# Grouped-query attention on one core: TensorE's whole program put into one loop, with a first turn in which every operation is jumped over

## The chip, the cores and the metric

One core of a Trainium2 chip runs the kernel. The metric is the device time of one execution in microseconds (us); smaller is better. Five engines work side by side, each through its own instruction stream, and wait for each other by semaphores: TensorE (PE; its weight loads are PEld), VectorE (DVE), ScalarE (ACT), GpSimd (POOL) and SyncE (SP), which here only issues transfers. Sixteen DMA engines move data between the device's memory and the on-chip buffers, and also bring the engines' instructions.

## What is computed

```python
B, Hq, Hkv, Sq, Sk, D = 16, 32, 8, 16, 2048, 128        # q, k, v in bfloat16
k = jnp.repeat(k, rep, axis=1)                          # rep = 4
v = jnp.repeat(v, rep, axis=1)
scores = jnp.einsum("bhqd,bhkd->bhqk", q, k) * D ** -0.5
p = softmax(scores, axis=-1)
return jnp.einsum("bhqk,bhkd->bhqd", p, v)
```

K and V are 67 MB each; every one of the 128 pairs of batch and KV head has 64 query rows (4 heads of 16).

## The kernel before

**Tiling.** Four (batch, KV head) pairs are a quad; there are `NQD` = 32 quads. A quad is worked in two steps of two pairs each, so there are `NT` = 64 steps. Four quads share one load of Q (`NQC` = 8). Per quad one K load of 2048 KB and two V loads of 1024 KB are made. K has 3 buffers (`NK`), V has 4 (`NV`), the probabilities transposed (`PT`) have 4, the output 8.

**A step on the engines.** VectorE transposes K blocks on the fly (`kt`, L450: two instructions of 1.2 us a step) into `KT`. TensorE's operation S (L362 to L375) multiplies them with the transposed Q into `S_ps`: 32 matmuls, 16 with a weight load of their own (L372) and 16 on weights already loaded (L317). VectorE negates, scales and takes the maximum (`negated`, L463), and makes the bias (L472). ScalarE takes exp into `P` (L579). TensorE's PT (L392) transposes `P` into `ST_ps` in 8 instructions, and ScalarE evicts them (L591). TensorE's PV (L421) multiplies with V into `O_ps`: 64 matmuls, each with a weight load. ScalarE scales the finished quad by the reciprocal sum ("norm", L602), POOL packs it (L198), and SP stores it. Q (L350) is TensorE's transposition of a new Q group, after VectorE or POOL has laid it out (L178), once in eight steps.

**TensorE's order.** `pe_step(p)` gives S of step p+2, a Q in one step out of eight, PV of step p-5 and PT of step p-1. The program has three parts: `head` (warm-up matmuls W of no use to the result, Q of group 0, and the steps that have no PV yet) as straight code; a loop of `TURNS` = 8 turns with eight steps each; and the PV of the last quad as straight code. The loop's first instruction is put on slot `HEAD` = 82 of a 256-instruction block of the code. Within the loop the semaphores' values come from registers set at the start of each turn (L434 to L436). `in_last` names the operations that the last turn has too; the others lie within `pe.If_lt(...)` and are jumped over then (L438). VectorE has a loop of its own for nine turns (L505).

**What orders the transfers.** SP works through a fixed list: for each t it issues a Q load, a K load (even t), V loads, and later stores. A wait at one of them holds back all that stand behind it. A K load of quad n waits until VectorE has transposed quad n-3 (L248). A V load of quad n waits until TensorE has done PV of quad n-4 (L255). The K loads of quads 0 to 2 wait for nothing; that of quad 3 (t = 6) waits for VectorE's first two `kt` pairs, which need no TensorE work; that of quad 4 (t = 8) waits for the transposes in VectorE's steps 0 and 1, each of which stands behind an S.

**The end.** The last quad's V comes in three transfers over the keys 0 to 15, 16 to 27 and 28 to 31 (`LASTV`, `sem_vl`), its PV goes to `S_ps` in place of `O_ps` (`o_ap`, L165 to L168), and the last norms are shared between VectorE and ScalarE.

Of the kernel before, what the change touches and what calls it, by code (L numbers as in the profile page):

```python
# [7 lines left out]
ALU = mybir.AluOpType  # L8
# [5 lines left out]
NV = 4  # L14
# [7 lines left out]
PVLAG = 5  # L22
# [4 lines left out]
TURNS = 8  # L27
HEAD = 82
WARM = (7, 22, 6, 6, 6)
RING = 6  # L30
NMBASE = 8
EXPBASE = 3
VLOOP = (3, 30)
VHEAD = 140
LASTV = ((0, 16), (16, 28), (28, 32))


def bass_standalone__gqa_softmax__sampling_kernel(
# [13 lines left out]
    assert NQD % 4 == 0 and PVLAG == 5 and 8 * TURNS == NT and NQC == TURNS  # L52
# [71 lines left out]
    def pe_step(p):  # L124
        ops = [("S", p + 2)]
        if p >= PVLAG and (p + 3) % 8 == 0:
            ops += [("Q", (p + 3) // 8, b) for b in range(2)]
        if p >= PVLAG:
            ops.append(("PV", p - PVLAG))
        if p >= 1:  # L130
            ops.append(("PT", p - 1))
        return ops

    head = [("W", 0), ("Q", 0, 0), ("Q", 0, 1), ("W", 1), ("S", 0), ("W", 2), ("S", 1), ("W", 3), ("S", 2), ("W", 4)]
    head += pe_step(0)[1:]
    for p in range(1, PVLAG):
        head += pe_step(p)
    L = NT - 4
    turn_ops = [op for p in range(PVLAG, PVLAG + 8) for op in pe_step(p)]

    def in_last(op):
        e = 8 * (TURNS - 1)
        if op[0] == "Q":
            return op[1] + TURNS - 1 < NQC
        return op[1] + e < (NT - 2 if op[0] == "PV" else NT)

    tail = [("PV", NT - 2), ("PV", NT - 1)]

    act_prog = [("qe", 0, 0), ("qe", 0, 1)]
    for p in range(NT - 3):  # L150
# [5 lines left out]
        if p >= 1:  # L156
# [3 lines left out]
                 ("pe", L + 3, 0), ("norm", NQD - 1, 0)]  # L160
# [4 lines left out]
    def o_ap(n, x):  # L165
        if n != NQD - 1:
            return O_ps[:, 512 * x:512 * x + 128]
        return S_ps[:, 512 * x:512 * x + 128]  # L168
# [33 lines left out]
    with nc.Block() as block:  # L202

        @block.gpsimd
        def _(gp):
# [18 lines left out]
            gp.tensor_tensor(fold[:, :, :], half_m[:, :, 0, :], half_m[:, :, 1, :], op=ALU.add).then_inc(sem_id, 1)  # L224
            gp.sem_inc(sem_nm, NMBASE)
# [18 lines left out]
        def _(sp):  # L244
# [6 lines left out]
            def load_v(p):  # L251
                n, c = divmod(p, 2)
                s = n % NV
                if n >= NV and c == 0:
                    sp.wait_ge(sem_pv, 2 * (n - NV) + 2)  # L255
                if n < NQD - 1:
                    dst = Vb[s][:, c, :, :].rearrange("a j d -> a (j d)")
                    sp.dma_start(dst, vf[p]).then_inc(sem_v[s][c], 16)
                    return
                if c == 0:  # L260
                    return
                for x, (lo, hi) in enumerate(LASTV):
                    dst = Vb[s][:, :, lo:hi, :].rearrange("a c j d -> a c (j d)")
                    src = vf[p - 1:p + 1, :, 128 * lo:128 * hi].rearrange("c a x -> a c x")
                    sp.dma_start(dst, src).then_inc(sem_vl[x], 16)
# [8 lines left out]
            def store(n):  # L274
                s = n % NO
                if n < PAIRED:
                    sp.wait_ge(sem_pc, 2 * n + 2)
                elif n < NQD - 2:
                    sp.wait_ge(sem_nm, NMBASE + 2 * n + 2)
                elif n == NQD - 2:  # L280
                    sp.wait_ge(sem_nl, 3)
                else:
                    sp.wait_ge(sem_nm, NMBASE + 2 * (NQD - 2) + 1)
                    sp.wait_ge(sem_nl, 4)
                for c in range(2 if n < NQD - 1 else 1):
                    store_part(sp, n, c)

            for t in range(NT + SLAG):
                if t == 4:
                    sp.sem_inc(sem_exp, EXPBASE)  # L290
                    sp.sem_inc(sem_e2, TURNS - 1)
                for c in range(NQC):
                    if t == (QLOAD[c] if c < len(QLOAD) else 8 * c - QLEAD):
                        load_q(c)
                if t < NT and t % 2 == 0:
                    load_k(t // 2)
                for p in range(NT):
                    if t == p + VLAG[p >= VFAR]:
                        load_v(p)
                if t >= SLAG and t % 2 == 0:  # L300
                    store((t - SLAG) // 2)
# [4 lines left out]
        def _(pe):  # L306
            regs = {}

            def wait(s, value, slope, turn):
                pe.wait_ge(s, regs[slope, value] if turn else value)  # L310

            def held(turn):
                if turn:
                    pe.wait_ge(sem_id, 10)
# [10 lines left out]
            def emit(op, turn=False):  # L325
                if op[0] not in ("PT", "W"):
                    held(turn)
                if op[0] == "W":
                    if op[1] == 0:
                        pe.wait_ge(sem_id, 3)  # L330
                    w = ident4[:, :].bitcast(BF16)
                    x = w.unsqueeze(1).to_broadcast([128, 2, 256])
                    dst = O_ps[:, 0:512].rearrange("p (t q) -> p t q", t=2)
                    pe.matmul(dst, w[:, 0:128], x, start=True, stop=True)
                    for _ in range(WARM[op[1]] - 1):
                        matmul_on_loaded(dst, w[:, 0:128], x, (0, 0), True, True, (128, 128))
                elif op[0] == "Q":
                    _, c, b = op
                    if b == 0:
                        if c == 0:  # L340
                            pe.wait_ge(sem_id, 10)
                        wait(sem_q4, 4 * c + 4, 4, turn)
                    if c >= 1:
                        wait(sem_ev[b], 8 * c - 4, 8, turn)
# [8 lines left out]
                elif op[0] == "S":  # L353
                    _, n = op
                    wait(sem_kt, n + 1, 8, turn)
                    if n >= 1:
                        wait(sem_max, n, 8, turn)
                    c, i = divmod(n // 2, 4)
                    if n % 8 == 0:
                        wait(sem_qe, 2 * c + 2, 2, turn)  # L360
# [15 lines left out]
                elif op[0] == "PT":  # L376
                    _, h = op
                    if h % 2 == 0:
                        wait(sem_exp, EXPBASE + h + 2, 8, turn)
                    if h % 8 == 7:  # L380
                        wait(sem_e2, h // 8 + 1, 1, turn)
                    for i in range(2):
                        if h >= 4 and h % 8 == 4:
                            if i == 0:
                                wait(sem_qe, 2 * (h // 8) + 4, 2, turn)
                        elif h >= 1:
                            wait(sem_ev[i], h, 8, turn)
# [6 lines left out]
                elif op[0] == "PV":  # L394
                    _, h = op
                    n, half = divmod(h, 2)
                    if h < NT - 2:
                        wait(sem_ev[1], h + 1, 8, turn)
                    else:
                        for i in range(2):  # L400
                            wait(sem_ev[i], h + 1, 8, turn)
                    if n < NQD - 1 and half == 0:
                        for c in range(2):
                            wait(sem_v[n % NV][c], 16 * (n // NV + 1), 16, turn)
                    if half == 0:
                        if n == NQD - 1:
                            wait(sem_max, NT, 8, turn)
                        else:
                            wait(sem_nm, NMBASE + 2 * n, 8, turn)
                    pt = PT[h % NPT][:, :, :].bitcast(BF16).rearrange("p t (c q e) -> p t e c q", c=2, e=2)  # L410
                    for j in range(16):
                        key = 16 * half + j
                        if n == NQD - 1:
                            for x, (lo, _) in enumerate(LASTV):
                                if key == lo:
                                    pe.wait_ge(sem_vl[x], 16)
# [10 lines left out]
            for op in head:  # L427
                emit(op)
            PE = mybir.EngineType.PE
            for slope, values in ((8, range(1, 21)), (16, (16,)), (4, (8,)), (2, (4,)), (1, (1,))):  # L430
                for value in values:
                    regs[slope, value] = pe.alloc_register(f"r_{slope}_{value}")
            with nc.Fori(0, TURNS, 1, engines=[PE], head_slot={PE: HEAD}) as m:
                for (slope, value), r in regs.items():  # L434
                    pe.reg_alu(r, m, slope, ALU.mult)
                    pe.reg_alu(r, r, value, ALU.add)  # L436
                for kept, ops in groupby(turn_ops, in_last):
                    with nullcontext() if kept else pe.If_lt(regs[8, 1], 8 * (TURNS - 1) + 1):  # L438
                        for op in ops:
                            emit(op, True)  # L440
            for op in tail:
                emit(op)

        @block.vector
        def _(dve):
# [29 lines left out]
            def step(n):  # L475
# [7 lines left out]
                if x == 1:  # L483
                    dve.wait_ge(sem_max, n + 1)
# [18 lines left out]
            r_n = [dve.alloc_register(f"r_n{x}") for x in range(6)]  # L503
            r_k = [dve.alloc_register(f"r_k{x}") for x in range(2)]
            with nc.Fori(V0 // 3, V1 // 3, 1, engines=[VE], head_slot={VE: VHEAD}) as i:  # L505
                dve.reg_alu(r_n[0], i, 6, ALU.mult)
                dve.reg_alu(r_n[0], r_n[0], 1, ALU.add)
                for x in range(1, 6):
# [4 lines left out]
                for n in range(6):  # L513
# [6 lines left out]
                    if x == 1:  # L520
                        dve.wait_ge(sem_max, r_n[n])
# [28 lines left out]
            dve.wait_ge(sem_e2, TURNS)  # L550
# [4 lines left out]
            norm(NQD - 2, (0, 1), sem_nl)  # L555
# [3 lines left out]
        def _(act):  # L559
            for op in act_prog:  # L560
# [31 lines left out]
                elif op[0] == "free":  # L592
                    act.wait_ge(sem_ev[1], op[1] + 1)
# [10 lines left out]
            act.wait_ge(sem_nm, NMBASE + 2 * (NQD - 2) + 1)  # L604
            act.wait_ge(sem_nl, 4)
# [29 lines left out]
```

## Time and profile before

| | |
|---|---|
| three runs | 337.61, 337.77, 337.82 us; median 337.77 |
| the profiled execution | 337.53 us; span of the trace 335.7 us |
| busy share of the span | DVE 92%, PE 83%, ACT 66%, PEld 47%, POOL 31% |
| `KT` on DVE (L450) | 128 instructions, mean 1218 ns |
| `Sneg` on DVE (L463) | 128 instructions, mean 1205 ns |
| TensorE's first matmul, first Q, first S | 1.86, 5.30, 11.64 us |
| Q, K and V loads, median from issue to landing | 16.1, 18.2, 21.4 us |
| last V loads issued | 315.96 to 317.9 us |

The profiled execution is one execution; its span runs from the first to the last record. A timeline row has the start, the time over all its instructions, engine and line, the operation with out<-in, the count (x), and in brackets the idle time before it and what ended it; "issue" means that the engine waited for nothing that the profile shows. A row of the issue list (SPq) is the time at which SP issues a transfer, not when it lands. A wait row has the time in total, the number of times and the longest. A queue row has packets, MB, and the time that its packets took as a share of sixteen DMA engines over the stretch asked for. Register, branch and semaphore instructions have no rows among the engines' work.

### The profile page before, as it was taken

The numbers are of one execution on the slowest core, as the hardware profiler recorded it, in microseconds if no ns is written. First come the engines' busy times: TensorE is split into PE (matmuls) and PEld (weight loads), VectorE is DVE, ScalarE is ACT, GpSimd is POOL, SyncE is SP. The second block draws the span as 40 slices with busy tenths as digits, with TensorE's granted clock in tenths as the row PEclk, the third lists the DMA queues.
The fourth block names the chain that finished last, engine by engine and source line by source line (L and its number), as shares of the span: only waits on it lengthen the run. The fifth ranks groups of instructions, "written<-read, shape, count | busy, mean of one in ns | idle before, by whom it ended". The sixth has DMA issues, their size and how long they took to land.

```text
span 335.7 us, 14448 instructions
## 1 busy us (share of the span) xinstructions
PE 280.0 (83%) x6959; PEld 158.3 (47%) x5893; DVE 308.0 (92%) x465; ACT 220.6 (66%) x331; POOL 104.1 (31%) x98
## 2 busy tenths in 40 slices
PE   7877678888988899888988898878877979777895
PEld 2013344445545555455644554444543545444575
DVE  1999998998999999999999999899999999999872
ACT  2044666766787677766777677756767757567671
POOL 3840037300680029400680029400592000000000
PEclk9999999999999999999999999999999999999999
DMA  7999999999999999999999999999999999999995
GB/s 293 443 418 428 424 416 412 423 424 426 415 420 418 424 431 422 423 428 417 414 428 427 424 424 414 422 427 429 422 419 420 423 427 428 420 427 412 422 411 177
DMA packets 21151, 138.62 MB, mean 413 GB/s; under 512 B 3728, under 2 KB 7568, under 8 KB 9104
## 3 DMA queue, kind: packets, MB, share of 16 engines
q1 hardware_dynamic: 20992, 138.39, 99.3%
q8 instruction: 9, 0.15, 0.2%
q10 hardware_dynamic: 144, 0.03, 0.1%
q14 instruction: 6, 0.05, 0.0%
HBM read 136.31 MB, written 2.10 MB: 412 GB/s over the span
## 4 chain that ended last, share of the span: by engine, by line
DVE 49%; DMA 28%; PE 17%; issue 3%; ACT 2%; DVEq 0%
DMA Kn<-in_k_dram 27%; DVE Sneg L463 25%; DVE KT L450 22%; PE S_ps L372 5%; PE S_ps L317 4%; PE O_ps L421 3%; PE ST_ps L392 2%; PE ST_ps L350 2%; ACT P L579 1%; PE O_ps L317 1%; DMA Qn<-in_q_dram 1%; PE S_ps L421 1%; DVE Q L178 1%; ACT PT L591 0%; DVE nbias L472 0%
## 5 line engine op out<-in xcount | busy, mean ns | idle before, releaser
L450 DVE STREAM_TRANSPOSE KT<-Kn 128x1024 f32<-128x1024 f32 x128 | 151.0, 1218 | 10.3 <-DMA Kn<-in_k_dram 10.3
L463 DVE TENSOR_SCALAR_CACHE_REDUCE Sneg<-S_ps 128x1024 f32<-128x1024 f32 x128 | 149.9, 1205 | 4.9 <-PE S_ps L317 4.4
L579 ACT ACTIVATE P<-Sneg,nbias 128x2048 bf16<-128x2048 f32 (+1 forms) x66 | 129.0, 1955 | 15.4 <-DVE nbias L472 15.2
L372 PE MATMUL S_ps<-KT,QT 32*64 32x512 bf16 x1024 | 106.5, 387 | 35.4 <-DVE Sneg L463 34.4
L591 ACT ACTIVATE PT<-ST_ps 128x512 f32<-128x512 f32 x123 | 66.7, 597 | 60.2 <-PE ST_ps L392 60.2
L317 PE MATMUL S_ps<-KT,QT 32*64 32x512 bf16 x1024 | 106.0, 381 | 0.0
L178 POOL TENSOR_SCALAR Q<-Qn,mask 128x1024 bf16<-128x1024 bf16 x28 | 79.2, 2842 | 48.3 <-PE ST_ps L350 42.2
L372 PEld LDWEIGHTS S_ps<-KT,QT 32*64 32x64 bf16 x1024 | 34.8, 103 | 104.3 <-issue 91.3
L421 PEld LDWEIGHTS O_ps<-Vb,PT 64*64 64x64 bf16 x3968 | 58.0, 107 | 49.1 <-issue 48.7
L421 PE MATMUL O_ps<-Vb,PT 64*64 64x128 bf16 x3968 | 67.9, 218 | 14.4 <-DMA Vb<-in_v_dram 12.4
L198 POOL COPY O<-O 32x256 bf16<-32x256 bf16 x56 | 22.0, 393 | 163.9 <-ACT O L602 145.7
L392 PE MATMUL ST_ps<-ident,P 128*128 128x128 f32 x512 | 69.9, 280 | 0.2 <-ACT P L579 0.2
L392 PEld LDWEIGHTS ST_ps<-ident,P 128*128 128x128 f32 x512 | 54.8, 141 | 8.4 <-issue 2.6
L602 ACT ACTIVATE O<-O_ps,rrec 128x128 bf16<-128x128 f32 x56 | 17.5, 363 | 22.1 <-PE O_ps L421 22.1
L567 ACT ACTIVATE QT<-ST_ps 128x512 bf16<-128x512 f32 x14 | 7.7, 595 | 9.1 <-PE ST_ps L350 9.0
L579 ACT ACTIVATION_READ_ACCUMULATOR P<-Sneg,nbias 128x1 f32 x66 | 13.3, 201 | 0.0
L350 PEld LDWEIGHTS ST_ps<-fold,Q 128*128 128x128 bf16 x256 | 8.5, 101 | 7.9 <-issue 7.9
L317 PE MATMUL O_ps<-ident 128*128 128x512 bf16 x42 | 11.2, 415 | 0.0
L463 DVE DVE_READ_ACCUMULATOR Sneg<-S_ps 128x1 f32 x128 | 10.5, 82 | 0.0
L350 PE MATMUL ST_ps<-fold,Q 128*128 128x32 bf16 x256 | 9.4, 198 | 0.3 <-DVE Q L178 0.3
L472 DVE TENSOR_TENSOR nbias<-nhalf 128x2 f32<-128x2 f32 x32 | 5.3, 167 | 1.1
L459 DVE RECIPROCAL rrec<-rowsum 128x2 f32<-128x2 f32 x31 | 4.9, 159 | 0.0
(27 smaller groups left out, 19.9 us busy)
## 6 DMA issues: line engine op xcount, KB each, us to landing
Kn<-in_k_dram SPq DMA_DIRECT2D x32, 2048.0 KB, 18.2
Vb<-in_v_dram SPq DMA_DIRECT2D x63, 1024.0 KB, 21.4
Qn<-in_q_dram SPq DMA_DIRECT2D x8, 256.0 KB, 16.1
out_dram<-O SPq DMA_DIRECT2D x63, 32.0 KB, 19.8
Vb<-in_v_dram SPq DMA_DIRECT2D x1, 768.0 KB, 14.4
Vb<-in_v_dram SPq DMA_DIRECT2D x1, 256.0 KB, 14.6
out_dram<-O ACTq DMA_DIRECT2D x1, 32.0 KB, 2.0
```

The source lines that it names most:

```text
L178: eng.tensor_scalar(Q4[:, :, :, r, :].rearrange("p j b x -> p (j b) x"), src, mask[:, r:r + 1], None, op0=ALU.mult,).then_inc(sem_q4, 1)
L198: eng.tensor_copy(Osb[n % NO][64 * c:64 * c + 32, :, 1, :], Osb[n % NO][64 * c + 32:64 * (c + 1), :, 0, :],).then_inc(sem_pc, 1)
L317: return pe.add_instruction(mybir.InstMatmult(name=nc.get_next_instruction_name(), engine=mybir.EngineType.PE, ins=[pe.lower_ap(rhs), pe.l ...
L350: ins = pe.matmul(dst[:, j // 2, j % 2, e], src[:, j, b, e, :], fold[:, :, :], start=True, stop=True)
L372: ins = pe.matmul(s_ap, w, x, start=(acc == 0), stop=(acc == 3))
L392: ins = pe.transpose(dst[:, 128 * z:128 * (z + 1)], src[:, t, :], ident4[:, :])
L421: ins = pe.matmul(o_ap(n, x)[64 * c:64 * (c + 1), :], w[rows, c], Vb[n % NV][rows, c, key, :], start=(key == 0), stop=(key == 31),)
L450: ins = dve.transpose(KT[n % NKT][:, :].rearrange("p (t b g e a) -> p e g t b a", t=8, b=2, g=2, e=2)[:, e], Kn[Q % NK][:, :].bitcast(F32) ...
L463: ins = dve.tensor_scalar(Sneg[p % NS][:, 1024 * x:1024 * (x + 1)].rearrange("p (t a m) -> p t a m", t=8, m=4), S_ps[:, 1024 * y:1024 * (y ...
L579: ins = act.activation(P[n % 2][:, lo:hi, x, :].bitcast(BF16), Sneg[p % NS][:, 128 * lo:128 * hi].rearrange("p (t k) -> p t k", k=128), AC ...
L591: act.activation(pt_ap(h, i), stage_ap(h, i), ACT.Copy).then_inc(sem_ev[i], 1)
L602: act.activation(Osb[n % NO][:, x, 0, :], o_ap(n, x), ACT.Copy, scale=col(rrec, 2 * n + x)).then_inc(sem_nm, 1)
```

## The change

1. `head` and the tail go into the loop. The loop now begins three steps earlier in each turn's order (S of step 8t-1, Q of group t, PV of step 8t-8, and so on), and the order of the operations that are carried out stays the same. Turn 0 carries out what was `head`, turn 8 what was the end. Operations that belong to the turn's own group of steps are jumped over when `ended` is set, those of the group before when `started` is not. The warm-ups stand within the loop and are carried out in turn 0 alone. The loop starts on slot 0 of a block of code.
2. The loop runs ten times. In the first time the turn number is 15 (m + 15, cut to four bits), which sets `ended` and clears `started`: every operation is jumped over. Then turns 0 to 8 follow.
3. Since every wait takes its value from a register now, semaphores are given a base: `sem_max` 1, `sem_ev` 8, `sem_vl` 112, `sem_e2` 7, added by POOL and SP at their start. Seven of eight S drop their wait on the transposed K (`sem_kt`), which the wait on `sem_max` implies.
4. The last quad's V comes in four transfers: keys 0 to 15 as two (one for each half of the quad, on `sem_v`), then 16 to 27 and 28 to 31 as before. Its PV goes to `O_ps` like all others, and so waits for both norms of quad 30; of these ScalarE now does one and VectorE one, where VectorE did both.

```diff
-TURNS = 8
-HEAD = 82
+TURNS = 9
+HEAD = 0
...
     def pe_step(p):
         ops = [("S", p + 2)]
-        if p >= PVLAG and (p + 3) % 8 == 0:
-            ops += [("Q", (p + 3) // 8, b) for b in range(2)]
...
+        if p == 2 - PVLAG:
+            ops += [("Q", 0, b) for b in range(2)]
+        return ops + [("PV", p - PVLAG), ("PT", p - 1)]
...
-    turn_ops = [op for p in range(PVLAG, PVLAG + 8) for op in pe_step(p)]
+    turn_ops = [op for p in range(2 - PVLAG, 10 - PVLAG) for op in pe_step(p)]
...
     def o_ap(n, x):
-        if n != NQD - 1:
-            return O_ps[:, 512 * x:512 * x + 128]
-        return S_ps[:, 512 * x:512 * x + 128]
+        return O_ps[:, 512 * x:512 * x + 128]
...
-                for x, (lo, hi) in enumerate(LASTV):
+                for y in range(2):
+                    sp.dma_start(Vb[s][:, y, 0:16, :].rearrange("a j d -> a (j d)"),
+                                 vf[p - 1 + y, :, 0:2048]).then_inc(sem_v[s][y], 16)
+                for lo, hi, done in ((16, 28, sem_vl[0]), (28, 32, sem_vl[1])):
...
-                    wait(sem_kt, n + 1, 8, turn)
-                    if n >= 1:
-                        wait(sem_max, n, 8, turn)
+                    wait(sem_max, MAXBASE + n, 8)
...
                     if n % 8 == 0:
-                        wait(sem_qe, 2 * c + 2, 2, turn)
+                        wait(sem_kt, n + 1, 8)
+                        wait(sem_qe, 2, 2)
...
-            for op in head:
-                emit(op)
...
-            with nc.Fori(0, TURNS, 1, engines=[PE], head_slot={PE: HEAD}) as m:
+            with nc.Fori(0, TURNS + 1, 1, engines=[PE], head_slot={PE: HEAD}) as m:
+                pe.reg_alu(turn, m, 15, ALU.add)
+                pe.reg_alu(turn, turn, 15, ALU.bitwise_and)
+                pe.reg_alu(ended, turn, 8, ALU.bitwise_and)
+                pe.reg_alu(started, turn, 7, ALU.add)
+                pe.reg_alu(started, started, 8, ALU.bitwise_and)
                 for (slope, value), r in regs.items():
-                    pe.reg_alu(r, m, slope, ALU.mult)
+                    pe.reg_alu(r, turn, slope, ALU.mult)
                     pe.reg_alu(r, r, value, ALU.add)
-                for kept, ops in groupby(turn_ops, in_last):
-                    with nullcontext() if kept else pe.If_lt(regs[8, 1], 8 * (TURNS - 1) + 1):
+                with pe.If_eq(regs[8, 1], 1):
+                    pe.wait_ge(sem_id, 3)
+                    warm_up(WARM[0])
+                for first, ops in groupby(turn_ops, lambda op: op[1] >= 0):
+                    with pe.If_eq(ended, 0) if first else pe.If_ne(started, 0):
                         for op in ops:
-                            emit(op, True)
-            for op in tail:
-                emit(op)
+                            emit(op)
+                            if op in warm:
+                                with pe.If_eq(regs[8, 1], 1):
+                                    warm_up(WARM[warm[op]])
...
-            norm(NQD - 2, (0, 1), sem_nl)
+            norm(NQD - 2, (1,), sem_nm)
             norm(NQD - 1, (1,), sem_nl)
```

## The prediction

> **What bounds the kernel now.** I read the busy shares first, then the chain of waits and the wait table, then the DMA queues stretch by stretch, then the timelines of SP and PE. From the page and its wait tables:
>
> ```profile
> DMA  7999999999999999999999999999999999999995
> HBM read 136.31 MB, written 2.10 MB: 412 GB/s over the span
> DVE 49%; DMA 28%; PE 17%; issue 3%; ACT 2%; DVEq 0%
> DVE KT L450 <- DMA Kn<-in_k_dram: 10.3, 11, 3.7
> SPq L249 <- DVE KT L450: 185.5, 29, 8.4
> ```
>
> The DMA engines are full from the second slice to the last but one: the span is a start of some 2 us, then 138 MB at about 0.425 MB/us, then a tail behind the last transfer. VectorE holds the largest share of the chain (49%), but it waits 10.3 us for K, all of it late: it is slightly faster than the transfers and catches up with them. The last row is the feedback that matters. A K load waits until VectorE has transposed the K block three quads back (L248), so a late VectorE can leave the queues empty, and bytes not moved then are lost for good.
>
> How far from empty are they? The DMA queues from 0 to 28 us (one row, nothing else in it), and the issue rows of SP:
>
> ```profile
> q1 hardware_dynamic: 1231, 10.87, 94.0%
> ...
> 13.47 0.33 SPq L249 DMA_DIRECT2D Kn<-in_k_dram  x1
> 13.84 0.91 SPq L258 DMA_DIRECT2D Vb<-in_v_dram  x2
> 23.12 0.33 SPq L249 DMA_DIRECT2D Kn<-in_k_dram  x1
> ```
>
> Before the issue at 23.12 (the fifth K) SP has asked for three Q of 256 KB, four K of 2048 KB and two V of 1024 KB: 0.79 + 8.39 + 2.10 = 11.27 MB. 10.87 MB are moved at 28.0, so at 0.425 MB/us the queues would be empty at 28.9. From the first issue at 0.72 to full flow takes about 1.8 us (2.37 MB in the first 8 us are 5.5 us at full rate). The margin is 28.9 - 23.12 - 1.8 = 4.0 us.
>
> **What code loading costs now.** The instruction queue q8 is TensorE's; the page has 9 packets of it, 0.15 MB, so 16.4 KB each. The stretches 50.9 to 52.4 and 76.6 to 78.1 hold one each (first two rows), 85 to 331 holds none (last row: q14 is another engine's). Beside it, TensorE's timeline:
>
> ```profile
> q8 instruction: 1, 0.02, 4.5%
> q8 instruction: 1, 0.02, 5.0%
> q14 instruction: 4, 0.03, 0.0%
> ```
>
> ```profile
> 51.09 0.97 PE L421 MATMUL O_ps<-Vb,PT 64*64 64x128 bf16 x53
> 53.42 0.36 PE L421 MATMUL O_ps<-Vb,PT 64*64 64x128 bf16 x11 [1.36 <-issue]
> ...
> 72.36 0.47 PE L421 MATMUL O_ps<-Vb,PT 64*64 64x128 bf16 x19 [0.74 <-issue]
> ...
> 79.64 0.41 PE L372 MATMUL S_ps<-KT,QT 32*64 32x512 bf16 x2 [0.89 <-issue]
> ```
>
> In the loop's first turn TensorE stops in the middle of an operation, waiting for no other engine, and starts again a little after a packet has come. From 72.36 to 79.64 it takes 19 PV matmuls with their weight loads (38 instructions), a PT (16), an S (48), a PV (128), a PT (16) and the first of an S: about 256 with the waits, one packet of code. So code comes a block at a time, a block is asked for only when the one before it is entered, and that took 79.64 - 72.36 = **7.28 us** here. The packet starts 76.6 or later, so at least 4.2 us went by ahead of it and at most 3.0 us from its start to the restart. After the first turn nothing is fetched: the loop stays.
>
> **The change, part by part.**
>
> *The jumped turn.* The loop holds per turn 8 S (48 each), 8 PV (128), 8 PT (16), Q (64), the warm-ups (47 matmuls, 5 loads): 1652, and some 70 waits, register and branch instructions, so 1720, 6.7 blocks. It starts on slot 0 of a block. In before the first q8 packet starts at about 29.1 us, after TensorE has passed its first 256 instructions (they end just ahead of the S at 25.50) and so entered its second block; two blocks are there at the start. So the jumped turn must fetch six more, each asked for when the one ahead is entered. TensorE starts at about 0.75. Block 2 comes when the queues are still nearly empty: 0.75 + 3.0 = 3.8. Then, at 7.28 each beside full queues: 11.0, 18.3, 25.6. The next is asked for at 25.6 and finds the queues empty at 28.9: 31.9, then 34.9. The last jumps, the back edge and the register set-up: 2 us (estimate; VectorE's loop back edge with its nine register instructions is a 0.68 us gap at 98.81 in the chain, and TensorE has over four times the registers). Warm-up starts at **36.9** instead of 1.86.
>
> The Trainium skill (Runtime: NRT & Kernel Launch, section "Instruction fetch mechanics") says that code is streamed in 16 KiB blocks and that the cost of crossing a boundary is mostly hidden; the packets of 16.4 KB agree, the stops of 1.36, 0.74 and 0.89 us do not. By that rule the turn would cost its branches alone, which is the second rival.
>
> *From there to the K load.* First warm-up to first S took 11.64 - 1.86 = 9.8 us, of which 0.3 was a wait on VectorE's Q, long done now: 9.5. First S to the fifth K's issue took 23.12 - 11.64 = 11.5 us, all on VectorE and TensorE. The issue falls at 36.9 + 9.5 + 11.5 = 57.9, data flows at 59.7, and the queues have been empty since 28.9: **30.8 us** lost. The fourth K (13.47) needs only the two transposes ahead of the first S and isn't delayed. Afterwards a quad takes VectorE 9.3 us and the queues 4.33 MB / 0.425 = 10.2, so they stay full to the end, with little backlog at first (up to 1 us more, kept for the range).
>
> *First-turn stops removed.* About 3 us of them lie in the chain; they are worth nothing, since VectorE has 10.3 us of K waits late in the run to lose first, and the queues were full while TensorE stood. Uncovered they would be worth those 3 us.
>
> *Fewer waits, more branches.* Seven of eight S lose their wait on the transposes; S starts 0.11 us after VectorE's row ends, so at most 0.11 each; some ten branches a turn are added, which TensorE's queued work hides. All this lies under the full queues: 0. Without that cover it is below 1 us a turn either way, and VectorE has the same 10.3 us of slack.
>
> *The last quad.* Its PV now writes O_ps, so it waits for quad 30's two norms:
>
> ```profile
> 328.01 2.13 PE L421 MATMUL O_ps<-Vb,PT 64*64 64x128 bf16 x128
> 330.28 0.61 DVE L535 TENSOR_SCALAR O<-O_ps,rrec 128x128 bf16<-128x128 f32 x2 [1.41 <-PE O_ps L421]
> 330.45 1.98 PE L421 MATMUL S_ps<-Vb,PT 64*64 64x128 bf16 x128 [0.32 <-issue]
> ```
>
> The norms are shared out: ScalarE's takes 0.37 (L602), VectorE's half of 0.61. From 330.28 that is 330.65, and with 0.1 for the signal TensorE starts at 330.75: **+0.3**. V's fourth transfer adds one issue of 0.47 us; the last part (issued by 316.9, 14.6 to land, 331.5) is needed at 330.45 + 28/32 of 1.98 = 332.2, so 0.7 us cover it; without that, 0.5. POOL's five extra semaphore instructions lie ahead of a Q that waits until 9.6 us anyway.
>
> *Sum.* Against the profiled execution (span 335.7, 337.53 with what lies around it; the median of the runs is 337.77): 337.5 + 30.8 + 0.3 = **368.6**.
>
> **Rivals.**
>
> *Fetches without the wait ahead of the packet.* If the 4.2 us come only from deep queues, and the start is not yet like that, a block costs 3.0: 0.75 + 6 x 3.0 + 2 = 20.8; first S 30.3, issue 41.8, flow 43.6, lost 14.7: **352.5**. For it: at the start fewer transfers are outstanding. Against: the share is full from 8 us on, and the first packet (29.1) came at least 3.6 us after its block was entered (ahead of the S at 25.50). Between the two cases any price from 3.0 to 7.28 is possible.
>
> *Not slower: the code is there.* If all of the loop is resident at launch or streams in ahead of the jumps, the turn costs its 19 taken jumps and registers. At 0.1 us a jump warm-up starts at about 5.5, 3.6 us late, inside the margin of 4.0, and the time is 337.5 + 0.3 = **337.8**; it turns slower as soon as warm-up starts after 5.9, and with 0.25 us a jump (a third of VectorE's back edge) it starts at 8.5 and loses 2.6: 340.4. For it: nothing is fetched in turns two to eight, so the space is there. Against: nine packets for ten blocks of program, with the first in the second block. The 0.1 is taken by the Trainium skill (Advanced Engine Details and Errata, section "Control Flow Timing", about 108 ns for a compare-and-branch); no row here lists a branch.
>
> *Dearer.* The emptied queues don't shorten the last fetches, or a jump into a block that is under way asks for it anew: 0.75 + 6 x 7.28 + 2 = 46.4, so 9.5 more: **378**.
>
> **Numbers.** Forecast 368.6, its own range 360 to 374: 0.68. Cheaper fetches, 345 to 360: 0.15. Code there: 0.08 (of it 0.03 faster, 0.03 within, 0.02 slower). Dearer: 0.09. The range is 352 to 377: it leaves out the code-there case (0.08), the lower part of the cheaper fetches (0.06) and half of the dearer case (0.05). About 0.2% (0.7 us) is what a measurement of this kernel can tell from no change. Faster 0.03, same 0.03, slower 0.94.
>
> **What would show it.** Right: six or seven q8 packets ahead of the first warm-up, some 7 us apart, then none; TensorE's first matmul at 30 to 40 us; the DMA share near zero from about 29 to 59 us and full after; the fifth K's issue near 58; no stops of TensorE in mid-operation later; 0.3 us more between the last two quads' PV. Wrong: a first matmul ahead of 10 us, or code packets close together, or queues that refill without a gap.

## The result, and the profile after

The changed kernel takes **367.35 us** (median of 6 runs, 366.46 to 368.39) where the kernel before takes 337.62 (337.51 to 337.82): 1.0881 times as long, 95% interval 1.0856 to 1.0906. The profiled execution took 368.0 us, with a span of 366.2. Of the runs in the experiments one (346.06 us, with 38 more warm-up matmuls) lay 1.5% above the fastest of its kernel, at a lower granted clock, and is left out of its time.

The changed kernel's page: busy share of the DMA engines and what they moved in 40 slices of 9.15 us, then TensorE's instruction queue, then the engines' shares of the chain.

```profile
DMA  8992007999999999999999999999999999999994
GB/s 315 425 417 88 0 0 262 422 424 422 426 423 413 421 423 425 427 423 425 418 430 416 424 421 422 416 421 427 426 422 429 424 422 422 420 418 424 420 412 122
q8 instruction: 7, 0.11, 0.1%
DVE 55%; PE 17%; DMA 13%; issue 12%; ACT 2%; POOL 1%; DVEq 0%; POOLq 0%
```

The hole in the fourth to seventh slice, with two slices at 0 GB/s, is nearly the whole story. On either side of it the queues run at the same 420 GB/s as before. "issue" has grown from 3% to 12% of the chain.

SP's issue rows and TensorE's first rows of the changed kernel:

```profile
14.65 0.33 SPq L239 DMA_DIRECT2D Kn<-in_k_dram  x1
...
56.64 0.33 SPq L239 DMA_DIRECT2D Kn<-in_k_dram  x1
```

```profile
35.49 0.60 PE L319 MATMUL O_ps<-ident 128*128 128x512 bf16 x1 [35.49 <-issue]
...
45.17 0.42 PE L357 MATMUL S_ps<-KT,QT 32*64 32x512 bf16 x4
```

TensorE runs no matmul for 35.49 us and waits for no engine in that time. Its first S starts at 45.17 (11.64 before), and the fifth K, which SP could ask for at 23.12 before, is asked for at 56.64. The wait behind it, and VectorE's for K:

```profile
SPq L239 <- DVE KT L438: 234.8, 29, 39.8
DVE KT L438 <- DMA Kn<-in_k_dram: 8.2, 7, 4.6
```

SP's longest wait for VectorE's transposes was 8.4 us and is 39.8 now.

What fills the 35.49 us stands in the trace's records of branches, which the views leave out. The jumped turn's 19 jumps run from 2.77 to 33.45 us. Thirteen of them take 0.21 to 0.25 us each; six take 1.91, 5.22, 5.64, 5.58, 5.74 and 2.68 us, 26.8 in all, and each of these six ends 2.3 to 2.6 us after a packet on q8 has started. At 0.21 us each the six would come to 1.3, so waiting for code is 25.5 of the 35.49 us.

The traffic of the changed kernel about the hole (per stretch the busy us of PE, PEld, DVE, ACT and POOL with the number of instructions, TensorE's granted clock, the share of the DMA engines, GB/s):

```profile
28.00:32.00 4.00, 0.00 (x0) 0.00 (x0) 0.00 (x0) 0.00 (x0) 0.00 (x0) 1.00 0.36 143
32.00:36.00 4.00, 0.51 (x2) 0.10 (x1) 0.00 (x0) 0.00 (x0) 0.00 (x0) 1.00 0.02 4
...
56.00:60.00 4.00, 2.65 (x34) 0.52 (x13) 4.00 (x7) 2.45 (x4) 0.00 (x0) 1.00 0.62 176
60.00:64.00 4.00, 2.46 (x36) 1.28 (x20) 3.96 (x8) 1.42 (x3) 0.00 (x0) 1.00 0.96 412
```

143 GB/s over 4 us are 1.35 us at full rate, so the queues run dry at 29.3; 176 are 1.66 us, so they flow again at 58.3: 29.0 us empty. In the trace's packets the last large transfer ends at 359.59, before at 330.30. That is 29.29 of the 30.43 us by which the span grew; the other 1.14 us are behind the last transfer:

```profile
357.61 2.26 PE L400 MATMUL O_ps<-Vb,PT 64*64 64x128 bf16 x128
360.52 1.09 PE L400 MATMUL O_ps<-Vb,PT 64*64 64x128 bf16 x64 [0.65 <-DVE O L523]
361.80 1.09 PE L400 MATMUL O_ps<-Vb,PT 64*64 64x128 bf16 x64 [0.18 <-issue]
```

From quad 30's PV to the end of the last PV it takes 362.89 - 357.61 = 5.28 us, before 332.43 - 328.01 = 4.42. The break ahead of the last quad is 0.65 (before 0.32), and the operations in the loop now stand 0.1 to 0.2 us apart where they followed at once. The other 0.3 of the 1.14 lie ahead of that: quad 30's PV starts 1.98 us ahead of the end of the last large transfer, 2.29 before.

### The profile page after: what moved, and what is told of

Same layout as the page of the kernel before. It is cut to its first block, busy times and chain, and to the rows that moved or that the text cites. A ratio compares the mean times of both kernels' runs of the same rounds, so it can differ in the third digit from the quotient of the medians.

```text
span 366.2 us, 14698 instructions
## 1 busy us (share of the span) xinstructions
PE 279.6 (76%) x6959; PEld 158.8 (43%) x5893; DVE 307.4 (84%) x464; ACT 221.5 (60%) x332; POOL 104.2 (28%) x98
## 4 chain that ended last, share of the span: by engine, by line
DVE 55%; PE 17%; DMA 13%; issue 12%; ACT 2%; POOL 1%; DVEq 0%; POOLq 0%
DVE Sneg L451 29%; DVE KT L438 25%; DMA Kn<-in_k_dram 13%; PE S_ps L357 4%; PE S_ps L307 3%; PE O_ps L400 3%; PE ST_ps L336 2%; PE ST_ps L377 2%; PE O_ps L307 2%; ACT P L567 1%; DVE rrec L447 0%; ACT PT L579 0%; DVE nbias L460 0%; PE O_ps L319 0%; DVE O L523 0%
## 5 line engine op out<-in xcount | busy, mean ns | idle before, releaser
L400 PEld LDWEIGHTS O_ps<-Vb,PT 64*64 64x64 bf16 x4096 | 59.7, 107 | 42.2 <-issue 41.9
L400 PE MATMUL O_ps<-Vb,PT 64*64 64x128 bf16 x4096 | 69.7, 217 | 7.8 <-DMA Vb<-in_v_dram 6.9
L590 ACT ACTIVATE O<-O_ps,rrec 128x128 bf16<-128x128 f32 x58 | 18.3, 364 | 24.6 <-PE O_ps L400 24.6
L319 PE MATMUL O_ps<-ident 128*128 128x512 bf16 x5 | 2.3, 461 | 35.5 <-issue 35.5
L307 PE MATMUL O_ps<-ident 128*128 128x512 bf16 x42 | 11.2, 415 | 0.0
```

What stands on the lines that cost most here:

```text
L307: return pe.add_instruction(mybir.InstMatmult(name=nc.get_next_instruction_name(), engine=mybir.EngineType.PE, ins=[pe.lower_ap(rhs), pe.l ...
L400: ins = pe.matmul(o_ap(n, x)[64 * c:64 * (c + 1), :], w[rows, c], Vb[n % NV][rows, c, key, :], start=(key == 0), stop=(key == 31),)
L590: act.activation(Osb[n % NO][:, x, 0, :], o_ap(n, x), ACT.Copy, scale=col(rrec, 2 * n + x)).then_inc(sem_nm, 1)
```

## Experiments

The theory: the jumped turn has to fetch six blocks of code one behind the other, TensorE and so VectorE start late, the fifth K is held back, and what the queues can't move then is lost. Nothing else in the change matters, but for the end. The rivals are named with each run. Times of the kernel before beside them were 337.5 to 337.6.

**Without the jumped turn.**

```diff
-            with nc.Fori(0, TURNS + 1, 1, engines=[PE], head_slot={PE: HEAD}) as m:
-                pe.reg_alu(turn, m, 15, ALU.add)
+            with nc.Fori(0, TURNS, 1, engines=[PE], head_slot={PE: HEAD}) as m:
+                pe.reg_alu(turn, m, 0, ALU.add)
```

> The changed kernel without its first, jumped turn (nine turns, the code not loaded ahead). Theory (the jumped turn is what costs, through the code blocks that it has to fetch): the first warm-up near 3 us, the first S at 12 to 14 us, stops of TensorE in mid-operation in turn 0 and none later, the fifth K issued at 23 to 26 us, the queues never empty, time 337.5 to 340. Rival (the branches and register waits of the big loop cost in every turn): 345 or more.

338.77 us, 1.0037 times before (1.0024 to 1.0051). First warm-up at 2.91, first S at 14.74, fifth K:

```profile
26.22 0.33 SPq L239 DMA_DIRECT2D Kn<-in_k_dram  x1
```

That is 3.1 us later than before and inside the margin of 4.0; the last large transfer ends at 330.37, as before (330.30). TensorE stops twice in mid-turn 0, for 0.40 us up to 31.0 and for 1.68 up to 36.8; both restarts come 2.5 to 2.8 us after the start of a packet on q8 (28.26 and 34.28). So all of the change but the jumped turn costs 1.2 us, and these lie behind the last transfer: the one loop, its branches and its bases cost the body of the run nothing.

**Two jumped turns.**

```diff
-            with nc.Fori(0, TURNS + 1, 1, engines=[PE], head_slot={PE: HEAD}) as m:
-                pe.reg_alu(turn, m, 15, ALU.add)
+            with nc.Fori(0, TURNS + 2, 1, engines=[PE], head_slot={PE: HEAD}) as m:
+                pe.reg_alu(turn, m, 14, ALU.add)
```

> Two jumped turns in place of one. Theory (the first pays for code blocks, the jumps themselves are cheap): the second finds its code there and costs some 7 us (19 jumps of about 0.27 us and the registers), all of it lost since the queues are empty by then: first warm-up near 42.5 us, no further packets on the instruction queue, time 373 to 376. Rival (a jump costs what the first turn shows, 33 us for 19 of them): first warm-up near 69 us, time near 400.

373.6 us (372.77 to 374.85), 6.3 more than with one. The queue q8 has seven packets, as with one turn, and the first warm-up comes at

```profile
40.86 0.60 PE L319 MATMUL O_ps<-ident 128*128 128x512 bf16 x1 [40.86 <-issue]
```

5.4 us later (the packets themselves came up to 1.6 us sooner in this run). By the branch records the second turn takes 7.1 us (31.9 to 38.9), with some 0.27 from one jump to the next and no record of one over 0.22; the first takes 31. So it is the fetching, not the jumping.

**One jump over the whole body.** In the first turn the body is skipped by a single branch; operations, blocks of code and turns are the same.

```diff
+                with pe.If_ne(turn, 15):
...
-                for first, ops in groupby(turn_ops, lambda op: op[1] >= 0):
+                    for first, ops in groupby(turn_ops, lambda op: op[1] >= 0):
```

> The changed kernel with one jump over the whole body in the first turn, in place of 19. Theory (what costs is that each block of code is asked for only when the one ahead is entered): only one or two blocks are fetched in the first turn, the first warm-up comes at 6 to 10 us, the other blocks are fetched during turn 0 as in the kernel without a jumped turn; time 338 to 342. Rival (a jumped turn waits until all code that it passes over is there): first warm-up near 35 us, 367.

343.87 us (342.57 to 344.46), some 2 us over the expected range. First warm-up:

```profile
11.07 0.60 PE L319 MATMUL O_ps<-ident 128*128 128x512 bf16 x1 [11.07 <-issue]
```

Only two packets of q8 lie ahead of it (at 2.9 and 6.5 us), the others come during turn 0. The fifth K is issued at 31.18, so 31.18 + 1.8 - 28.9 = 4.1 us are lost and 1.1 at the end: 342.7 by the theory's sum, against 342.57 in the profiled run, which is the fastest of the four. My 6 to 10 us for the first warm-up was too short for two fetches, the registers and a second pass of the loop's head. A jumped turn doesn't wait for all the code that it passes over: the one jump takes 6.1 us by its record, the 19 of the changed kernel together 30.7. That it waits only for the blocks that it sets foot in, and with 19 landings sets foot in all, fits this but isn't shown further: the trace doesn't say which blocks the two packets brought, and q8 has nine packets in this run where the changed kernel has seven.

**K held back.** SP asks for the second K only when the first half of TensorE's first Q is done, so the queues are empty during most of the jumped turn.

```diff
             def load_k(n):
                 s = n % NK
+                if n == 1:
+                    sp.wait_ge(sem_stq, 1)
```

> The changed kernel with the second and all later loads of K (and what stands behind them on SP) held until TensorE's first Q is done, so that the queues are empty from about 8 us on while the jumped turn fetches. Theory (a block costs some 6 us beside full queues and 3.2 beside empty ones; what is lost is the time in which the queues are empty): packets on the instruction queue some 3.2 us apart, first warm-up at 22 to 25 us, queues empty from 8 to about 28 us, time 355 to 359, so faster than the changed kernel although transfers are held back. Rival (a block costs 6 us whatever the traffic): first warm-up at 35 us, queues empty for some 30 us, 367 or more.

362.51 us (361.88 to 362.58): 4.8 us *faster* than the changed kernel although it starts its transfers later, but 3.5 us above the expected range. The packets of q8 start at 3.2, 8.7, 12.2, 15.2, 18.2, 21.2 and 24.2, so 5.5 us apart while the first K flows and 3.0 to 3.4 after it; in the changed kernel they start at 3.2, 8.7, 14.9, 21.1, 27.2, 30.3 and 33.6, so 5.5 to 6.2 apart beside full queues and 3.1 to 3.3 about the moment at which those run dry (29.3). What I had wrong is the release:

```profile
26.16 0.60 PE L321 MATMUL O_ps<-ident 128*128 128x512 bf16 x1 [26.16 <-issue]
...
29.98 0.85 SPq L241 DMA_DIRECT2D Kn<-in_k_dram  x2
```

From the first warm-up to that half of Q it takes 3.8 us more, which my sum left out. Empty from 8.6 to 29.98 + 1.8 = 31.8 are 23.2 us, and 337.5 + 23.2 + 1.1 = 361.8. With that the theory's account holds.

The branch records say where a fetch's time goes. The long jumps end 2.3 to 2.6 us after their packet's start in both kernels. From the end of one long jump (the next block entered) to the next packet's start it is 3.2 to 3.8 us beside full queues, and 0.65 to 1.1 beside empty ones. So the difference lies ahead of the packet. In this run's last four packets the start follows the entry steadily, by 0.65 to 0.78 us, and not the jump that needs the block, as it would if a block is asked for when the one ahead of it is entered.

**V ahead of the fifth K.**

```diff
-                    if t == p + VLAG[p >= VFAR]:
+                    if t == (7 if 2 <= p < 2 * NV else p + VLAG[p >= VFAR]):
```

> The changed kernel with the V loads of quads 1 to 3, which wait for nothing, issued ahead of the fifth K (6.3 MB more for the queues while TensorE jumps). Theory (what is lost is the time in which the queues are empty): 6.3 MB are 14.8 us of traffic, so the queues run dry near 44 instead of 29 us; TensorE starts 1 to 4 us later, since one or two more blocks of code come beside full queues; time 353 to 357. Rival (VectorE's late start sets the end): VectorE's start isn't earlier, so 367 or more.

367.23 us (366.39 to 368.96): no gain, as the rival had it. Here the theory in its simple form fell. The 6.3 MB did move while TensorE jumped, but look at the traffic after the hole:

```profile
48.00:56.00 8.00, 5.67 (x67) 1.18 (x33) 7.97 (x13) 1.15 (x1) 4.39 (x2) 1.00 0.00 0
56.00:64.00 8.00, 5.18 (x62) 1.55 (x28) 7.97 (x12) 4.01 (x6) 0.00 (x0) 1.00 0.70 262
64.00:72.00 8.00, 6.03 (x80) 2.83 (x48) 8.00 (x11) 5.73 (x8) 0.00 (x0) 1.00 0.56 207
72.00:80.00 8.00, 4.84 (x72) 1.99 (x40) 7.96 (x14) 5.68 (x8) 0.00 (x0) 1.00 0.62 218
80.00:88.00 8.00, 7.48 (x216) 5.18 (x196) 7.82 (x14) 5.79 (x11) 6.45 (x4) 1.00 0.58 197
88.00:96.00 8.00, 7.42 (x206) 4.35 (x171) 7.96 (x12) 5.57 (x8) 5.66 (x2) 1.00 0.98 415
```

From 56 to 88 us the queues run at half rate: one K per 9.3 us, and no V, since the V buffers are full until TensorE has done the first quad's PV (next V issue at 86.29). What was moved ahead is missing there. The bytes that may have moved by a given time are those that the buffers hold beyond what VectorE and TensorE have used up; the order of the list hardly changes them. By 88 us this run has moved 24.8 MB and the changed kernel 23.8, a lead of 2.2 us, of which 1.6 are left at the last large transfer of the profiled runs (357.99 against 359.59); the medians, 0.1 us apart in ranges of 2 us, don't show it. TensorE's first matmul comes 1.5 us later (37.03, since the last two blocks come beside full queues), its first S 0.5 us later (45.65). So "empty queues are lost time" needs the addition: the loss is set by how late the engines that free the buffers are, and an empty queue at the start is only where it first shows.

**TensorE late, nothing else.** Three runs of the kernel *before*, with a later first S and no jumped turn. First, 38 more matmuls in the warm-up:

```diff
-WARM = (7, 22, 6, 6, 6)
+WARM = (45, 22, 6, 6, 6)
```

> The kernel before with 38 more matmuls in the first warm-up: no other code, no jumped turn, TensorE's first S 8 to 10 us later. Theory (beyond a margin of 4.0 us every microsecond of delay is a microsecond of empty queues): time = 337.6 + delay - 4.0, so 341.6 for 8 and 343.6 for 10. Rival (VectorE's 10.3 us of late K waits take up the delay): no change, 337.6.

340.84 to 342.33 us in three runs, 1.0115 times before (1.0096 to 1.0133). First S at 19.05, 7.4 us late, a little less than the 8 to 10 expected; fifth K at 30.52, also 7.4 late. Theory: 337.6 + 7.4 - 4.0 = 341.0. The traffic:

```profile
28.00:32.00 4.00, 3.39 (x38) 0.66 (x17) 3.96 (x8) 3.76 (x3) 0.00 (x0) 1.00 0.62 174
32.00:36.00 4.00, 3.02 (x40) 1.42 (x24) 4.00 (x5) 0.80 (x3) 0.00 (x0) 1.00 0.80 328
```

At 425 GB/s it falls short by 3.3 us here, which is the theory's 3.4; another 0.9 us are missing from 72 to 76, behind a stop of TensorE for code (2.00 us at 60.57). VectorE's 10.3 us of K waits didn't take up the delay.

Second, 8 more matmuls (`WARM = (15, ...)`):

> The kernel before with 8 more matmuls in the first warm-up: TensorE's first S 1.5 to 2.5 us later. Theory (delays within the margin of 3 to 4 us are free): no change, 337.4 to 337.9. Rival (there is no margin, each microsecond counts): 339.1 to 340.1.

339.03 us, 1.0041 times before (1.0027 to 1.0055), with a first S only 1.05 us late. The expectation failed. TensorE's timeline shows where:

```profile
48.08 0.64 PE L372 MATMUL S_ps<-KT,QT 32*64 32x512 bf16 x4 [4.60 <-DVE KT L450]
```

It stands for 4.6 us at the loop's entry, though the transposes named as releaser were long done, and then runs at a granted clock of 0.50 (48 to 52 us; 1.00 before). The instruction queue has 10 packets in place of 9, one of them at 44.4, between stop and restart. The branch records settle what TensorE waits for: the jump into the loop takes 6.04 us (40.85 to 46.89), where it takes 0.31 in the kernel before. The loop head must stand on slot 82 of a block; eight more instructions ahead of it push it, by this reading, past slot 82 and so into the next block, which has to be fetched when the loop is entered. The run with 38 more has 10 packets too, and its jump into the loop takes 2.52 us. The lower clock has a small part in the 1.5 us: the two of the five runs with a mean granted clock of 1.00 took 338.64 and 338.82 us, the other three (0.984 to 0.989) 339.03 to 339.14. Third, therefore, a late start without one instruction more:

```diff
                     if op[1] == 0:
-                        pe.wait_ge(sem_id, 3)
+                        pe.wait_ge(sem_id, 10)
```

> The kernel before, its first warm-up waiting for the last of POOL's setup operations (near 4.1 us) in place of the third: TensorE's first S about 2 us later, with not one instruction more, so that the loop stays in the block of code where it was. Theory (a delay within the margin of 4.0 us is free; the 1.5 us of the run with eight more matmuls came from its loop head, which the eight instructions pushed into the next block): nine packets on the instruction queue, fifth K issued near 25, time 337.3 to 337.9. Rival (the margin is smaller, and late starts cost from the first microsecond): 339 or more.

337.65 us, 1.0001 times before (0.9992 to 1.0010), nine packets, a jump into the loop of 0.19 us, first S at 13.71 (2.1 us late), and

```profile
25.18 0.33 SPq L249 DMA_DIRECT2D Kn<-in_k_dram  x1
```

Two microseconds of delay are free, 3.1 in the kernel without a jumped turn are free as well, 7.4 cost 3.3 at this place. The margin of about 4 us stands. That the eight instructions shift the loop into the next block is read from the packet count and the long jump; no run moved the loop head by itself.

**The end alone.** The kernel before with O_ps for the last quad, the shared norms and the four transfers:

```diff
-        if n != NQD - 1:
-            return O_ps[:, 512 * x:512 * x + 128]
-        return S_ps[:, 512 * x:512 * x + 128]
+        return O_ps[:, 512 * x:512 * x + 128]
...
-            norm(NQD - 2, (0, 1), sem_nl)
+            norm(NQD - 2, (1,), sem_nm)
```

> The kernel before with the change of the last quad alone: last PV into O_ps behind both norms of quad 30, the norms shared out, last V in four transfers. Theory (the wait on the norms costs 0.3 us, the jumps between the last PVs in the loop the other 0.5 that the changed kernel's end is longer): from the start of quad 30's PV to the end of the last PV 4.7 to 4.8 us (before 4.43, the changed kernel 5.28), time 337.8 to 338.1. Rival (all of the longer end comes from the norms): 5.2 to 5.3 us, time 338.4 or more.

337.76 us, 1.0011 times before (1.0002 to 1.0020).

```profile
327.91 2.13 PE L417 MATMUL O_ps<-Vb,PT 64*64 64x128 bf16 x128
330.68 1.98 PE L417 MATMUL O_ps<-Vb,PT 64*64 64x128 bf16 x128 [0.64 <-DVE O L531]
```

332.66 - 327.91 = 4.75 us: the wait on the norms costs 0.33, as forecast. Both halves of the last PV run through without a break (1.98), so the other 0.53 of the changed kernel's 5.28 come with its loop: in each of the gaps between its last PVs stand two branches (records of 0.21 and 0.08 us) and waits; no run took these out alone.

No version here beats the kernel before. With the jumped turn gone the last transfer ends where it did, so preloaded code has nothing to win as long as the transfers set the end.

## Why the prediction was right

- **What bounds the kernel** (full queues, with a feedback from VectorE to the K loads): right, and the step that carried the forecast. The empty time was forecast as 30.8 us and measured as 29.0 (29.3 by the end of the last large transfer); 1.4 of the 1.8 too many come from the first warm-up, 0.4 from the time at which the queues run dry. The margin of 4.0 us is borne out by three late starts. Incomplete in one point: the loss can't be bought back by issuing other loads first.
- **Six blocks, one behind the other**: seven packets (the seventh is asked for on entering the last block), five of them ahead of 28 us, none after 34. First warm-up forecast at 36.9, found at 35.49. Two of its terms were mis-sized and offset each other. A block beside full queues was priced at 7.28, the stretch between two stops; it costs 5.5 to 6.2. The profile before had this: its packets from 51.04 to 83.62 us are 6.2, 6.4, 6.3, 7.2 and 6.4 apart, and I took the longest. And the first packet, which I let arrive by 3.8, starts only at 3.2, 2.4 us after TensorE, and the jump that waits for it ends at 5.53. What follows the sixth block (jumps, back edge, registers), estimated at 2 us, took 2.6 (32.90 to 35.49). The price for empty queues (3.0) was close to the 3.1 to 3.3 measured. One reading behind it was too firm: the first packet of the kernel before, at 29.13, needn't have waited 3.6 us. In the run of the end alone, with the same code up to there and the first S at 11.59, it starts at 24.19, ahead of the S at 25.46.
- **The Trainium skill's rule** (Runtime: NRT & Kernel Launch, section "Instruction fetch mechanics") that block crossings are mostly hidden, stated for a next block that is fetched while the current one is carried out, would have given the second rival, 337.8 to 340.4. The packets 5.5 to 6.2 us apart in the jumped turn and the 367.35 us speak against it here: jumped code has almost no work of its own to hide a fetch behind. Where the code is carried out, in the same loop without a jumped turn, the two stops in mid-turn come to 2.1 us, so there the rule is near.
- **From warm-up to the K load**: 9.5 + 11.5 = 21.0 forecast; 56.64 - 35.49 = 21.15.
- **First-turn stops, fewer waits, more branches at nothing**: right; without the jumped turn the last large transfer ends at 330.37 against 330.30. Their cover has an end, though: a stop of 4.6 us at the loop's entry cost the run with eight more matmuls 1.5 us.
- **The last quad, +0.3**: the norms' share is 0.33 as forecast. The term was mis-sized by the jumps between the last PVs, which I had put at nothing behind TensorE's queued work; at the end there is no such cover, and they cost 0.53. All of the end is 1.14 us longer, 0.8 more than forecast, and makes up for part of the 1.8 us by which the empty time came out shorter: that the sum is within 1.3 us of the 367.35 is partly luck.
- **The rivals**: code that is there, and a jumped turn of jumps alone, fall with the two jumped turns (6.3 us for the second) and with the six long jumps. The price of a jump in the first of them, 0.1 us, was too low as well: it is 0.27 from one to the next. With all code there the first warm-up would have come near 35.49 - 25.5 = 10.0 us, 8.1 late, and the time near 337.5 + 4.1 + 0.3 = 342 (an estimate), so slower even then. Cheaper fetches apply where the queues are empty, as the K held back shows, but not at a start at which the K loads are under way. The dearer case didn't occur: fetches did get shorter as soon as the queues ran dry.

## What to carry to other kernels

In this kernel code is fetched through the same DMA engines as the data, and waits behind it: before loading it ahead, ask what it will wait behind, how many blocks are asked for one behind the other, and what stands still in the meantime. When an engine that frees buffers starts late, first find the margin until the transfer queues run dry; up to there the delay is free, beyond it every microsecond is lost, and reordering the loads doesn't bring it back. When a timing experiment adds instructions ahead of a loop, check that it didn't move the loop's code as well.

## What the runs showed of the hardware

In the jumped turns a 16 KB block of TensorE's code took 5.5 to 6.2 us from one packet to the next beside full queues and 3.0 to 3.4 beside empty ones, so about half of a fetch is waiting behind other traffic: 3.2 to 3.8 us from entering a block to the next packet, against 0.65 to 1.1. A taken branch of TensorE took 0.21 to 0.25 us with its code there (0.27 from one to the next), and up to 5.74 where the code had to come. The loop's seven blocks stayed resident over nine turns: no packet on q8 from 34 us to the end. When TensorE stood still for 4.6 us in the run with eight more matmuls, its granted clock was 0.81 in the stretch from 44 to 48 us, 0.50 from 48 to 52 and 0.83 from 52 to 56; the S behind the stop took 3.6 us (48.08 to 51.71), where one takes 2.0 at full clock.
